# An attention layer fused with a mixture of attention experts: the start and the planner's rules reworked

## The chip, the cores and the metric

The kernel runs on one core of one Trainium2 chip. The metric is the device time of one execution in microseconds (us): 501.53 us before the change, the median of 3 runs (500.11 to 502.16). Five engines work side by side: TensorE (PE in the profile, with PEld for its weight loads), VectorE (DVE), ScalarE (ACT), GpSimd (POOL) and SyncE (SP), which only issues DMAs. ACT issues DMAs too.

## What is computed

Two layers follow each other for each of 8 batches: an attention with 8 heads, 512 local positions and 32 global ones, and a mixture of 4 experts, each of which is a causal attention over the 544 positions.

```python
# 1: attention; local queries see a band of 32 positions on each side, and the 32 global keys
s_g = scale * q_g @ concat(k_g, k_l).T;  out_g = softmax(s_g) @ concat(v_g, v_l)
s_ll = where(|i - j| <= 32, scale * q_l @ k_l.T, -1e9)
out_l = softmax(concat(scale * q_l @ k_g.T, s_ll)) @ concat(v_g, v_l)
x = concat(out_g, out_l), heads side by side        # 8 x 544 x 512

# 2: experts; two of the four are used at each position, by the gate's logits
logits = x @ w_gate;  w = softmax over the two largest
for e in range(4):
    q, k, v = x @ wq[e], x @ wk[e], x @ wv[e]
    out += w[e] * softmax(causal(scale * q @ k.T)) @ v @ wo[e]
```

All is fp32; the experts' products are taken in fp32r with operands split in a high and a low part.

## The kernel before

**Its units.** The attention goes by pairs of heads, four pairs to a batch, 32 pairs in all. A pair k passes through `p1_load` and `p1_load_values` (its keys, queries and values, `kn`, `qn`, `v`), `p1_trans` (keys and queries turned, on TensorE for the first 6 pairs, on DVE afterwards, into `kd` and `qp`), `p1_scores` (L536), `p1_softmax` (L548 on DVE, L551 on ACT), `p1_ptrans` (the weights turned by TensorE, L569), `p1_av` (the value product, L599) and `p1_turn` (L569 again, then `xh` and `xl`, the high and low part of x). Two pairs share the products of the global queries: `p1_global_scores` (L663) and `p1_global_av` (L703). The values need copies of their 32-row blocks to other partitions, `move` and the copies of `vg` in `p1_load_values`; all of them ran on POOL (L279 there).

When the four pairs of a batch are done, the experts follow: `m_v` (L762), `m_qk` (L733), the scores (L854), their turn (L569), the value product `m_av` (L921) and `out_tile` (L1003). `project` puts `m_v` of batch 0 into step 5 and the products of its queries and keys into steps 6 and 7, while the attention of batch 1 goes on.

**What sets the order.** No engine chooses at run time. Each function records operations in a `Plan` with a time that the author wrote down, and `Plan.place` then lays them out, always the one that can start first by its own account; on PE it weighs a penalty for a changed shape of the tile on the array (`CHANGE`) and one for late priority (`PULL`), over all operations within `REACH` of the first one. The priorities are 100 per step s. The order is then fixed, engine by engine, and an engine waits where the order's next operation is not ready.

**What can hold a queue.** A DMA that fills a buffer waits on its issuing engine until the buffer is free, and what is queued behind it waits too. `kn` and `qn` have three buffers each, `v` three, `vg` one; the expert weights come in through the buffers `mptw`, three of them. `setup` loads a weight and splits it in a high and a low part (one copy on ACT or DVE, one subtraction on DVE at L394). `setup_bands` and `setup_masks` build the constants; `load` issues on SP or ACT for the first step and on SP afterwards.

```python
for name, when in (("masks", 3), ("v", 2), ("k", 2), ("q", 3), ("o", 6)):
    if s == when:
        setup(name)
```

## Time and profile before

| | |
|---|---|
| median of 3 runs | 501.53 us (500.11 to 502.16) |
| the profiled execution, its own time | 505.81 us |
| its span, first to last instruction | 504.0 us |
| mean granted TensorE clock | 0.99 |
| chain that ended last | PE 76%, DVE 9%, DMA 4%, "issue" 4%, SP's queue 4%, ACT 3% |
| read from HBM, written to it | 30.42 MB, 8.91 MB |

The profile is of one execution. Its rows give a start or a busy time in us; "x64" is a count of instructions, and the brackets behind a row tell how long the engine had been idle and what ended that, "issue" where no semaphore did. A fp32 product is two matmul records, so that `p1_scores` with 32 matmuls in the program is 64 in the trace. Matmul and weight load are two instructions of one stream.

### The profile page before, as it was taken

To read this page: it belongs to the slowest core of one execution; us is meant where nothing else is said; L and a number is where in the kernel's file an instruction comes from. 1 tells how busy PE (TensorE), PEld (TensorE's weight loads), DVE (VectorE), ACT (ScalarE), POOL (GpSimd) and SP (SyncE) were. 2 spreads that over 40 slices of the span, in tenths; PEclk is the share of its full clock that TensorE was granted. 3 is DMA by queue.
4 is the path that set the end of the run, shared out by engine and by line. 5 is a ranking of instruction groups with operands and counts; after the bars stand their busy time and mean duration, and the time that the engine had idled before them with its cause. 6 is when DMAs were issued, how large, how long until landed. Compare 5 with 4: busy or idle time off the path is not lost.

```text
span 504.0 us, 25622 instructions
## 1 busy us (share of the span) xinstructions
PE 469.3 (93%) x10532; PEld 410.7 (81%) x10532; DVE 385.7 (77%) x1708; ACT 324.4 (64%) x1171; POOL 281.0 (56%) x520
## 2 busy tenths in 40 slices
PE   5787979799999999999989999999999999999985
PEld 3676968589889889889878889898988889888774
DVE  5889768989876997779956998769966976475570
ACT  1668636976756866768746867669757764563662
POOL 5879817869456492928656392837649261331220
PEclk9989989999999999999999999999999999999989
DMA  9955666654246324445146234453022100200203
GB/s 191 220 117 97 140 113 122 115 81 85 35 86 158 68 40 76 106 93 100 32 88 149 49 64 66 108 115 79 4 53 86 28 4 3 85 3 1 86 3 104
DMA packets 181620, 40.98 MB, mean 81 GB/s; under 512 B 176896, under 2 KB 176896, under 8 KB 181504
## 3 DMA queue, kind: packets, MB, share of 16 engines
q1 hardware_dynamic: 169488, 28.70, 31.0%
q10 hardware_dynamic: 12016, 10.65, 6.9%
q8 instruction: 82, 1.34, 1.1%
q14 instruction: 34, 0.28, 0.2%
HBM read 30.42 MB, written 8.91 MB: 78 GB/s over the span
## 4 chain that ended last, share of the span: by engine, by line
PE 76%; DVE 9%; DMA 4%; issue 4%; SPq 4%; ACT 3%; ACTq 1%; POOLq 0%; POOL 0%; DVEq 0%
PE bank L733 18%; PE bank L569 10%; PE bank L1003 9%; PE bank L762 8%; PE bank L921 7%; PE bank L599 6%; PE bank L854 5%; PE bank L536 4%; SPq L295 4%; DVE pm L868 3%; PE bank L703 2%; PE bank L663 2%; DMA qn<-in_q_l_dram 2%; DVE st L548 2%; PE bank L773 1%
## 5 line engine op out<-in xcount | busy, mean ns | idle before, releaser
L886 POOL TENSOR_SCALAR pm<-pm,msm,gate 128x512 f32<-128x512 f32 (+3 forms) x124 | 74.3, 612 | 101.1 <-DVE msm L877 56.1
L279 POOL COPY v<-v 32x512 f32<-32x512 f32 (+1 forms) x192 | 114.5, 596 | 19.8 <-DMA v<-in_v_l_dram 10.0
L551 ACT ACTIVATE st<-st,sm 128x128 f32<-128x128 f32 x256 | 99.7, 392 | 12.3 <-DVE sm L548 12.0
L279 POOL COPY v<-vg 32x640 f32<-32x640 f32 (+1 forms) x96 | 65.3, 680 | 37.6 <-PE bank L703 32.8
L872 ACT ACTIVATE pm<-pm,msm 128x512 f32<-128x512 f32 (+3 forms) x128 | 70.8, 554 | 18.9 <-DVE msm L868 17.8
L548 DVE CUSTOM_DVE_ANT_0 st<-bank,band 128x128 f32<-128x128 f32 x256 | 58.0, 284 | 3.2 <-PE bank L536 3.0
L868 DVE CUSTOM_DVE_ANT_0 pm<-bank,cmask 128x512 f32<-128x512 f32 (+3 forms) x128 | 55.2, 480 | 2.4 <-PE bank L854 2.1
L551 ACT ACTIVATION_READ_ACCUMULATOR st<-st,sm 128x1 f32 x256 | 48.6, 190 | 0.0
L854 PE MATMUL bank<-kt,qt 64*32 64x384 f32 (+3 forms) x1024 | 43.7, 433 | 1.0 <-issue 1.0
L921 PE MATMUL bank<-mptw,vt 128*64 128x128 f32 x640 | 41.0, 281 | 1.7 <-DVE xn L603 0.9
L599 PEld LDWEIGHTS bank<-v,ptw 128*32 128x32 f32 x2048 | 31.3, 112 | 12.8 <-issue 7.7
L536 PE MATMUL bank<-kd,qp 64*32 64x128 f32 x2048 | 39.4, 280 | 2.1 <-issue 2.1
L599 PE MATMUL bank<-v,ptw 128*32 128x64 f32 x2048 | 36.8, 223 | 4.4 <-DVE msm L868 2.5
L277 ACT COPY mptw<-bank 128x384 f32<-128x384 f32 (+1 forms) x50 | 24.2, 520 | 25.6 <-PE bank L921 18.4
L921 PEld LDWEIGHTS bank<-mptw,vt 128*64 128x64 f32 x640 | 36.6, 140 | 3.7 <-issue 2.3
L536 PEld LDWEIGHTS bank<-kd,qp 64*32 64x32 f32 x2048 | 32.1, 108 | 8.6 <-issue 5.0
L733 PE MATMUL bank<-xh,wk_hi 128*128 128x272 f32 x128 | 37.7, 294 | 0.0
L277 ACT COPY ptw<-bank 128x512 f32<-128x512 f32 x34 | 20.0, 594 | 27.1 <-PE bank L569 26.6
L733 PE MATMUL bank<-xl,wk_hi 128*128 128x272 f32 x128 | 37.0, 289 | 0.0
L733 PE MATMUL bank<-xl,wq_hi 128*128 128x272 f32 x128 | 36.9, 288 | 0.0
L733 PE MATMUL bank<-xh,wk_lo 128*128 128x272 f32 x128 | 36.9, 288 | 0.0
L733 PE MATMUL bank<-xh,wq_hi 128*128 128x272 f32 x128 | 36.8, 288 | 0.0
(159 smaller groups left out, 1321.1 us busy)
## 6 DMA issues: line engine op xcount, KB each, us to landing
out_dram<-ot ACTq DMA_DIRECT2D x32, 256.0 KB, 2.1
v<-in_v_l_dram SPq DMA_DIRECT2D x60, 120.0 KB, 2.9
kn<-in_k_l_dram SPq DMA_DIRECT2D x104, 64.0 KB, 2.8
qn<-in_q_l_dram SPq DMA_DIRECT2D x104, 64.0 KB, 2.8
v<-in_v_l_dram SPq DMA_DIRECT2D x31, 64.0 KB, 3.2
kn<-in_k_l_dram SPq DMA_DIRECT2D x8, 128.0 KB, 4.1
qn<-in_q_l_dram SPq DMA_DIRECT2D x8, 128.0 KB, 3.8
ot<-in_q_g_dram SPq DMA_DIRECT2D x8, 64.0 KB, 2.2
```

The source lines that it names most:

```text
L279: ENG[e].tensor_copy(out, in_)
L536: nc.tensor.matmul(sp[h].t[32 * g:32 * g + 32, 128 * t:128 * t + 128], qp.t[rows, 32 * u:32 * u + 32], kd.t[rows, c:c + 128], start=True, ...
L548: op("DVE", 211, lambda e, h=h, t=t, i=i: nc.vector.tensor_tensor_reduce(out=st.t[:, h, t], in0=sp[h].t[:, 128 * t:128 * t + 128], in1=ban ...
L551: op("ACT", 385, lambda e, h=h, t=t, i=i: nc.scalar.activation(st.t[:, h, t], st.t[:, h, t], AF.Exp, bias=sm.t[:, 0, i:i + 1], scale=-1.0, ...
L569: nc.tensor.transpose(two[y].t[:, k, :], block()[rows], ident[rows, rows])
L599: nc.tensor.matmul(xq.t[32 * g:32 * g + 32, t, h, :], pt.t[:, h, 32 * u:32 * u + 32], v.t[:, h, window(u), :], start=True, stop=True)
L733: nc.tensor.matmul(pp.t, w[:, ch, cols], x(part, ch)[:, n], start=(ch == 0 and w is hi and part == 0), stop=(ch == NCH - 1 and part == 1))
L854: nc.tensor.matmul(sp[x].t[32 * u:32 * u + 32, at:at + n], qt.t[rows, q0:q0 + 32], kt.t[rows, :n], start=True, stop=True)
L868: op("DVE", 78 + 1.04 * n, lambda e, x=x, at=at, n=n, i=i, s=s: nc.vector.tensor_tensor_reduce(out=pm.t[:, x, at:at + n], in0=sp[x].t[:, a ...
L872: op("ACT", 280 + 0.83 * n, lambda e, x=x, at=at, n=n, s=s: nc.scalar.activation(pm.t[:, x, at:at + n], pm.t[:, x, at:at + n], AF.Exp, bia ...
L886: lambda e, x=x, at=at, n=n, i=i, s=s: ENG[e].tensor_scalar(pm.t[:, x, at:at + n], pm.t[:, x, at:at + n], sm.t[:, 3, s:s + 1], gate.t[:, i ...
L921: nc.tensor.matmul(yp.t[64 * x:64 * x + 64, 128 * i - n0:128 * i - n0 + 128], vt.t[:, j, 64 * (2 * c + x):64 * (2 * c + x) + 64], flat[:, ...
```

## The change

The planner is changed in four ways. On PE it no longer takes the candidate with the least start time plus penalties, but the one that leaves least time unused, looking one operation further (`waste`, `DEPTH` 1). The penalty for a changed shape falls from 300 to 50 and the reach rises from 130 to 250. `run` keeps account of the instruction stream in blocks of 256, each of which comes a given time after a place in the block before the last. And between 14 and 45 us by its own clock, loads are ordered with less in flight (`FEW`).

```diff
+    def run(self, t, o, state):
+        shape, at, came, then = state
+        ns = o.ns["PE"] * (FILLX if t < SLOW else 1.0)
+        if o.shape != shape:
+            ns += SWITCH.get(shape, 95.0)
+        end, left = t, o.size
+        while left:
+            part = min(left, (LEAD if at < LEAD else BLOCK) - at)
+            end += ns * part / o.size
+            at, left = at + part, left - part
+            if at == LEAD:
+                then = max(end, came) + (FETCH if end > SLOW else FIRST_FETCH)
+            elif at == BLOCK:
+                end, came, at = max(end, came), then, 0
...
+    def waste(self, found, first, now, state, depth):
+        def cost(f):
+            t, o = max(f[0], now), f[1]
+            end, after = self.run(t, o, state)
+            c = end - now - o.ns["PE"] + CHANGE * (o.shape != state[0]) + PULL * (o.prio - first)
...
-                        t = max(t, lanes[0], dma - AHEAD)
+                        t = max(t, lanes[0], dma - (AHEAD if dma < FULL or dma > SLOW else FEW))
```

In the kernel itself six things change.

```diff
-            op("DVE", 1450, f, r=[tri], w=[("band", t)])
+            op("DVE" if t < 2 else "POOL", 1450 if t < 2 else 2200, f, r=[tri], w=[("band", t)])
...
-        op("POOL", 3750, f, w=["masks"])
+        op("POOL", 3750, f, r=[("w", "v")], w=["masks"])
...
+    def warm(after, n, ns):
+        def f(e):
+            nc.tensor.matmul(warm_to.t[:, :128 * n], ident, ident.unsqueeze(1).to_broadcast([128, n, 128]),
+                             start=True, stop=True)
+        op("PE", ns, f, r=after, w=[(warm_to, plan.prio)], size=4)
+    def start_tables():
+        first = buf("sgm", [128, 8], 3)
+        op("ACT", 1300, lambda e: nc.scalar.copy(first.t, ident[:, :8]), w=[first], late=40)
...
-        evac(lambda: kq.t, lambda: pg.t, 256, [pg], [kq])
+        evac(lambda: kq.t, lambda: pg.t, 256, [pg], [kq], "ACT|DVE" if b else "DVE")
...
-            return "POOL", ns
+            return ("POOL|ACT", (ns, 60 + 0.83 * n)) if k < SHARED else ("POOL", ns)
...
+    warm([], 4, 1700)
     p1_batch(0)
...
+    start_tables()
     p1_batch_turn(0)
+    warm([G[0]["pg"]], 1, 430)
     p1_trans(0)
+    warm([PR[0]["px"]], 1, 300)
     setup_bands()
...
-        for name, when in (("masks", 3), ("v", 2), ("k", 2), ("q", 3), ("o", 6)):
+        for name, when in (("masks", 3), ("v", 2), ("k", 2), ("q", 3), ("o", 8)):
```

`warm` multiplies the identity with itself on TensorE, to no use of the result. `start_tables` makes ACT load its function table before its first real work. The first copies out of the banks of pair 0 go to DVE alone, two of the four bands to POOL, and the copies of the values of the first 4 pairs (`SHARED`) may go to ACT. The masks wait for the value weights, so that they are built later. The output weights are loaded in step 8 and not in step 6. The scores, softmax and turning of the first four pairs get the priority of their own pair (`first`).

The planner lays out all 500 us anew. Three places show what the prediction speaks of. The first is TensorE's queue from its start; `ot` holds the global keys and queries, `kd` and `qp` the turned keys and queries. Before:

```order
L420 MATMUL bank_64<-ident,ot 128x64 x4
L506 MATMUL bank_65<-ident,kn 128x128 x4
L506 MATMUL bank_66<-ident,qn 128x128 x4
L506 MATMUL bank_67<-ident,kn 128x128 x4
L506 MATMUL bank_68<-ident,qn 128x128 x4
L536 MATMUL bank_69<-kd_77,qp 32x128
```

and with the change:

```order
L447 MATMUL bank_64<-ident 128x512
L477 MATMUL bank_65<-ident,ot 128x64 x4
L447 MATMUL bank_64<-ident 128x128
L565 MATMUL bank_66<-ident,kn 128x128 x4
L565 MATMUL bank_67<-ident,qn 128x128 x4
L447 MATMUL bank_64<-ident 128x128
L565 MATMUL bank_68<-ident,kn 128x128 x4
L565 MATMUL bank_69<-ident,qn 128x128 x4
L595 MATMUL bank_70<-kd_77,qp 32x128
```

Three products of the identity stand ahead of and between the turns; the first score product still stands behind the turned keys and queries of pair 1.

The second place is SP's queue from the expert weights on (`mptw` is the buffer that they come in through; the first `v` in each piece is that of pair 3, the first `vg` that of batch 1). Before:

```order
L295 DMA mptw<-in_moe_wk_dram 128x8x64 x2
L295 DMA kn<-in_k_l_dram 128x4x64 x2
L295 DMA qn<-in_q_l_dram 128x4x64 x2
L295 DMA mptw<-in_moe_wq_dram 128x8x64 x2
L295 DMA v<-in_v_l_dram 96x5x64 x2
L295 DMA v<-in_v_l_dram 128x2x64
```

and with the change:

```order
L339 DMA mptw<-in_moe_wk_dram 128x8x64 x2
L339 DMA kn<-in_k_l_dram 128x4x64 x2
L339 DMA v<-in_v_l_dram 96x5x64
L339 DMA vg<-in_v_g_dram 32x8x64
L339 DMA v<-in_v_l_dram 96x5x64
L339 DMA v<-in_v_l_dram 128x2x64
L339 DMA qn<-in_q_l_dram 128x4x64 x2
L339 DMA mptw<-in_moe_wq_dram 128x8x64 x2
```

The queries of pair 5 and the query weights have moved behind the values of pair 3 and the global values of batch 1. The first of these waits for a buffer of `v`, which is free when the first global value product (L703) has read the values of pair 0.

The third place is the high part of the output weights, `wo_hi`. Before it was copied on ACT, ahead of the gate's exponential (L830), the copies of projected keys and queries and of turned weights:

```order
L776 COPY vt<-bank_71 32x260
L277 COPY kt<-bank_66 128x272
L277 CAST wo_hi<-mptw 128x1024
L830 ACTIVATE xt<-xt 128x20
L277 COPY kt<-bank_70 128x272
L277 COPY qt<-bank_68 128x272
L277 COPY ptw<-bank_69 128x8x64
```

Now it is copied on DVE, in step 9, behind the turned queries (L578) of pair 9 and between small steps of the experts' softmax:

```order
L935 TENSOR_SCALAR msm<-msm 128x2
L578 STREAM_TRANSPOSE qp<-qn 128x512
L937 RECIPROCAL msm<-msm 128x2
L323 CAST wo_hi<-mptw 128x1024
L928 ISA pm,msm<-bank_71,cmask 128x128
L928 ISA msm 128x1
L438 TENSOR_TENSOR wo_lo<-mptw,wo_hi 128x1024
```

Its DMA now stands on SP behind 95 loads where it stood behind 69. On TensorE the whole order changes too: the expert products of a batch, which stood in runs of four, now stand in ones and twos between the products and turns of the pairs. Counted over the program, the shape of the tile on the array changes 233 times where it changed 178 times, and before the first `m_v` the instruction stream is 2076 instructions long (matmuls, weight loads and semaphore waits) where it was 2169: the score product of pair 6 has moved behind it.

More of the change, by code (lines that the diff above doesn't have):

```diff
@@ L68 @@
 MARGIN = 400.0
-REACH = 130
+REACH = 250
 PULL = 4.0
-CHANGE = 300.0
+CHANGE = 50.0
+THEN = 1.0
+DEPTH = 1
 SOON = 100
+SHARED = 4
+APART = 100
+EARLY = 0
+FILLX = 1.05
+BLOCK = 256
+FETCH = 3650.0
+FIRST_FETCH = 5000.0
+LEAD = 208
 class Plan:
@@ L124, in slot_time @@
         return t
+    def run(self, t, o, state):
[12 more added lines that the diff above has]
+                end, came, at = max(end, came), then, 0
+        if not o.size:
+            end = t + ns
+        return end, (o.shape, at, came, then)
+    def waste(self, found, first, now, state, depth):
[3 more added lines that the diff above has]
+            c = end - now - o.ns["PE"] + CHANGE * (o.shape != state[0]) + PULL * (o.prio - first)
+            if depth:
+                rest = [g for g in found if g is not f]
+                if rest:
+                    c += THEN * self.waste(rest, first, end, after, depth - 1)[0]
+            return c
+        return min(((cost(f), f[1].k, f) for f in found), key=lambda x: x[:2])
     def place(self, log=None):
+        state = (None, BLOCK - 193, 0.0, 0.0)
         free = dict.fromkeys(self.ENGINES, 0.0)
@@ L131, in place @@
         lanes = [0.0] * LANES
-        shape = None
         def enter(o):
@@ L142, in place @@
         left = len(self.ops)
+        last = (None, None)
         while left:
@@ L166, in place @@
                 if e == "PE":
-                    t, o = min(found, key=lambda f: (
-                        f[0] + CHANGE * (f[1].shape != shape) + PULL * (f[1].prio - pe[0].prio), f[1].k))
+                    key = (free[e], tuple((f[0], f[1].k) for f in found))
+                    if key != last[0]:
+                        last = key, self.waste(found, pe[0].prio, free[e], state, DEPTH)[2]
+                    t, o = last[1]
                 else:
@@ L181, in place @@
                     queue[x].remove(o)
-            ns = o.ns[e]
-            if e == "PE" and t < SLOW:
-                ns *= 1.3
-            if e == "PE" and o.shape != shape:
-                ns += SWITCH.get(shape, 95.0)
-                shape = o.shape
-            end = t + ns
+            if e == "PE":
+                end, state = self.run(t, o, state)
+            else:
+                end = t + o.ns[e]
             free[e] = end
@@ L500, in p1_trans @@
         if k < FIRST:
+            engs = "ACT|DVE" if k else "DVE"
             for src in (kn, qn):
-                px = ps([128, SL], "px")
+                px = pr["px"] = ps([128, SL], "px")
                 def f(e, src=src, px=px):
@@ L538, in f @@
                                          start=True, stop=True)
-        op("PE", 885, f, r=[qp, kd], w=sp, shape="scores")
+        op("PE", 885, f, r=[qp, kd], w=sp, shape="scores", size=128)
     def p1_softmax(k):
@@ L569, in f @@
                     nc.tensor.transpose(two[y].t[:, k, :], block()[rows], ident[rows, rows])
-        op("PE", 50 + 62 * n, f, r=r, w=two, shape="turn")
+        op("PE", 50 + 62 * n, f, r=r, w=two, shape="turn", size=4 * n)
         for y in range(2):
@@ L663, in f @@
                             nc.tensor.matmul(to, kq.t[rows, 2 * g + j, SG:], k_, start=True, stop=True)
-            op("PE", 704 - 480 * half, f, r=[kq, *kdl], w=[sp], shape="scores")
+            op("PE", 704 - 480 * half, f, r=[kq, *kdl], w=[sp], shape="scores", size=32)
             op("DVE", 78 + 1.04 * n, lambda e, sp=sp, half=half, n=n: nc.vector.tensor_scalar(
@@ L749, in clear @@
                 nc.gpsimd.memset(vt.t[64:128, 4, :], 0.0)
-            op("POOL", 720, clear, w=[(vt, "clear")])
+            op("POOL", 720, clear, r=[("w", "v")], w=[(vt, "clear")])
             for g in range(NCH // 2):
@@ L855, in f @@
                                          kt.t[rows, :n], start=True, stop=True)
-        op("PE", 20 + 1.68 * sum(128 * (i + 1) for i, _ in TILES[t]), f, r=[kt, qt], w=sp, shape="scores")
+        op("PE", 20 + 1.68 * sum(128 * (i + 1) for i, _ in TILES[t]), f, r=[kt, qt], w=sp, shape="scores",
+           size=32 * len(TILES[t]))
     def m_softmax(b, c, t):
@@ L924, in m_av @@
             op("PE", 214 * sum(i + 1 for i in some), f, r=[vt, *{id(pts[i][0]): pts[i][0] for i in some}.values()], w=[yp],
-               shape="half")
+               shape="half", size=8 * sum(i + 1 for i in some))
             high_low(lambda part, n0=n0, n=n: y[part].t[:, c, n0:n0 + n], lambda yp=yp: yp.t, n, [yp],
@@ L945, in f @@
                                      start=True, stop=True)
-            op("PE", 30 + 1.67 * n, f, r=[*qts, *kts], w=[sp], shape="scores")
+            op("PE", 30 + 1.67 * n, f, r=[*qts, *kts], w=[sp], shape="scores", size=16)
             if half == 0:
@@ L1060, in sooner, with first @@
         if k < NP:
-            plan.prio, then = 100 * k + SOON, plan.prio
+            plan.prio, then = APART * k + SOON, plan.prio
+            f(k)
+            plan.prio = then
+        else:
+            f(k)
+    def first(k, f):
+        if k < NP:
+            plan.prio, then = APART * k, plan.prio
             f(k)
@@ L1083, in local @@
             if at(s):
-                p1_scores(s)
-                p1_softmax(s)
+                first(s, p1_scores)
+                first(s, p1_softmax)
         def experts():
@@ L1119, in step @@
         if at(s + 1):
-            p1_trans(s + 1)
+            first(s + 1, p1_trans)
         if s < LAG:
```

45 lines of the change are left out of this document (26 added, 19 removed).

## The prediction

> **What bounds the kernel now.** First the share of busy time and the stages (each row: the stretch in us, its length, then busy time and count of PE, PEld, DVE, ACT and POOL, the granted clock, the DMA share and GB/s).
>
> ```profile
> PE 469.3 (93%) x10532; PEld 410.7 (81%) x10532; DVE 385.7 (77%) x1708; ACT 324.4 (64%) x1171; POOL 281.0 (56%) x520
> ...
> 0.00:11.00 11.00, 4.82 (x20) 3.36 (x20) 6.77 (x39) 2.12 (x3) 5.53 (x27) 1.00 1.09 187
> 11.00:23.00 12.00, 10.88 (x322) 8.79 (x320) 9.34 (x48) 7.75 (x37) 10.37 (x17) 1.00 1.17 218
> 23.00:32.00 9.00, 5.80 (x142) 5.01 (x142) 6.90 (x31) 5.99 (x23) 7.48 (x13) 0.81 0.77 155
> 32.00:51.00 19.00, 15.87 (x600) 12.65 (x597) 18.23 (x73) 12.86 (x51) 16.26 (x26) 1.00 0.53 96
> ...
> 66.00:75.00 9.00, 5.80 (x194) 5.08 (x196) 6.42 (x19) 3.10 (x9) 1.42 (x3) 0.81 0.61 99
> ...
> 105.00:480.00 375.00, 367.51 (x8132) 324.49 (x8134) 291.64 (x1275) 251.72 (x894) 202.99 (x371) 1.00 0.31 68
> ```
>
> From 105 to 480 us PE stands idle for only 7.5 of 375 us: there only PE's own work counts. What a better start can give lies ahead of that: up to 51 us, where the experts begin, and around 66 to 75, where PE is busy for 5.80 of 9 us. From 32 to 51 VectorE is the full engine, 18.23 of 19.
>
> Next PE's waits (sum in us, times, longest).
>
> ```profile
> PE bank L569 <- DVE xn L603: 3.6, 2, 3.2
> ...
> PE bank L569 <- issue: 2.6, 2, 2.2
> ...
> PE bank L536 <- issue: 2.1, 4, 1.1
> PE bank L599 <- issue: 1.8, 3, 0.8
> ...
> PE bank L984 <- issue: 1.4, 1, 1.4
> ...
> PE bank L854 <- issue: 1.0, 1, 1.0
> ...
> PE bank L703 <- issue: 0.9, 1, 0.9
> ...
> PE bank L921 <- issue: 0.7, 2, 0.5
> ```
>
> The seven rows with "issue" add up to 10.5 us: PE waited for no semaphore. The timeline says where (start, busy time, then the idle time before it).
>
> ```profile
> 11.19 1.96 PE L536 MATMUL bank<-kd,qp 64*32 64x128 f32 x64
> ...
> 25.71 0.34 PE L569 MATMUL bank<-ident,xn 64*128 64x64 f32 x4 [2.19 <-issue]
> ...
> 31.88 0.53 PE L703 MATMUL bank<-v,longt 96*32 96x64 f32 x20 [0.88 <-issue]
> ...
> 35.61 0.44 PE L536 MATMUL bank<-kd,qp 64*32 64x128 f32 x12 [0.26 <-issue]
> ...
> 38.30 0.87 PE L536 MATMUL bank<-kd,qp 64*32 64x128 f32 x41
> 39.78 0.64 PE L536 MATMUL bank<-kd,qp 64*32 64x128 f32 x23 [0.61 <-issue]
> ...
> 51.11 0.39 PE L762 MATMUL bank<-wv_hi,xh 128*128 128x260 f32 x1
> ...
> 69.72 0.46 PE L569 MATMUL bank<-ident,xn 64*128 64x64 f32 x8 [3.20 <-DVE xn L603]
> ```
>
> These waits cut through the middle of an operation: the product that goes on at 31.88 had stopped after 20 of its 40 matmuls, that of 38.30 after 41 of 64. Counted in matmuls and weight loads, they lie 256 instructions apart or a multiple of that. So I read them as PE waiting for its own program, which comes by DMA, to share the rings with the data. The DMA rows of 15 to 30 us and of 30 to 50 us (packets, MB, share) show its pace.
>
> ```profile
> q8 instruction: 3, 0.05, 1.4%
> ...
> q8 instruction: 5, 0.08, 1.8%
> ```
>
> A block of 256 every 5 us in the first, in which the data queue is full, and every 4 us in the second. Without waits, 600 matmuls and their 597 loads ran in 19 us, 4.06 us per 256: PE eats its program about as fast as it comes. The 82 blocks of the whole program (two instructions to each of 10532 matmuls, by 256) are not to be made fewer by this change.
>
> In the Trainium skill, "Runtime: NRT & Kernel Launch", section "Instruction fetch mechanics", the sequencer refills in blocks of 256 instructions by its own DMA queue, and the fetch is hidden, as it issues more slowly than it fills. The spacing agrees; that it is hidden does not, with 2.19 us at 25.71. By that rule the planner's account of blocks would win nothing.
>
> **The change, part by part.**
>
> *Fill: the first expert product (L762, 51.11).* The first scores stand at 11.19, behind the queries of pair 1. These are now issued earlier, behind ACT's table load, so I take the scores 1.5 us earlier. The identity, the first copies on VectorE and the two bands on POOL lie in PE's, VectorE's and POOL's waits for the first data, and I put them at nothing by themselves: PE and VectorE waited for DMAs there. The warm products may raise the clock sooner. The same four turns before and after the clock rose:
>
> ```profile
> 4.55 1.12 PE L506 MATMUL bank<-ident,kn 128*128 128x128 f32 x4 [0.45 <-DMA kn<-in_k_l_dram]
> ...
> 16.26 0.66 PE L506 MATMUL bank<-ident,kn 128*128 128x128 f32 x4
> ```
>
> At 1.12/0.66 for all PE work of 4.5 to 11 us (4.82 us busy at most by the first stage's length) and part of the first scores (1.96 against 1.12 in the row at 222.84 below), at most 2.5 us go; none if the block that comes next sets the pace, as at 25.71. I take 0, the nearest row being that wait. The first copies of pair 0 on VectorE cost at most one 0.6 us copy in a row.
>
> In the Trainium skill, "TensorE: Matmul & The Clock Gate", Part 1 wants about 3.4 us of sustained work for the full clock, while Part 4 has it that transposes don't count as busy as other products do. By Part 4 the warm products would bring up the clock where the turns can't: up to those 2.5 us; by the row at 25.71, nothing. The granted clock of 0.81 in 23 to 32 us, after 3.2 us of PE idle in all, agrees with Part 1; which of the two holds for turns no row tells.
>
> From then on VectorE sets the earliest end: 9.34 + 6.90 + 18.23 = 34.5 us of work from 11 to 51, and by the order its work before the first expert product stays within 1 us of that. From 11 us (scores 1.5 us earlier and their 1.3 us) with 1 us of gaps this gives 46.5. ACT has 7.75 + 5.99 + 12.86 = 26.6 us and gets 16 copies of values from POOL, less the cast of `wk_hi`:
>
> ```profile
> L277 ACT COPY ptw<-bank 128x512 f32<-128x512 f32 x34 | 20.0, 594 | 27.1 <-PE bank L569 26.6
> ...
> L279 POOL COPY v<-v 32x512 f32<-32x512 f32 (+1 forms) x192 | 114.5, 596 | 19.8 <-DMA v<-in_v_l_dram 10.0
> ```
>
> By 594 ns of the nearest ACT copy the 16 are at most 9.5 us, some smaller, less 1.1: 8, so 34.6 from 9.7, or 44.3. POOL falls from 34.1 us by as much and takes the bands early, so it is not last. PE's blocks: 2076 instructions instead of 2169, 93 fewer or 1.5 us at 4.06 us per 256, so 51.11 becomes 49.6 if no wait for a block goes, and earlier with lighter DMA in 14 to 45. From both sides: 51.1 (nothing) and 44.3 (ACT alone). I take 46.5 by VectorE's row, **−4.6**.
>
> What the moved loads add is a wait: SP's loads of pair 3's values stand behind the first global value product, with `vg` of batch 1, the queries of pair 5 and `wq` behind them. Before:
>
> ```profile
> 32.41 4.42 SPq L295 DMA_DIRECT2D v<-in_v_l_dram  x6
> ```
>
> That wait ended at 32.41, when the product at 31.88 was through. The product has moved in PE's stream from instruction 1002 to 1385, and stands before the products of pair 3; before, number 1385 ran at 38.3. If it runs at 33, as the 46.5 implies, nothing is late; if at 38.3, `v`, the queries of pair 5 and `wq` are 6 us late, and the gain is gone (rival 2).
>
> *Output weights two steps later.*
>
> ```profile
> 64.57 1.05 ACT L277 CAST wo_hi<-mptw 128x1024 fp32r<-128x1024 f32 x1 [4.53 <-DMA mptw<-in_moe_wo_dram]
> ```
>
> ACT stood 4.53 us for a load that was still under way, the gate's exponential behind it; VectorE's gates and `xn` followed, and PE stood 3.20 us at 69.72. Then the clock: 0.81 over the 9 us from 66, a loss of 0.19 x 9 = 1.7. Now VectorE casts in step 9, with more steps between its load and its use than before. Both go: **−4.9**. If the cast again waits for its load, VectorE stands in ACT's place, at most 3 us of it back; the other end is −4.9 in full, since the work of the cast is the same.
>
> *Steady state.* One score product moved behind the first expert product: +1.1 by its row (222.84). Then 55 more changes of shape (178 to 233). Pairs of rows:
>
> ```profile
> 185.36 1.13 PE L854 MATMUL bank<-kt,qt 64*32 64x512 f32 x14
> 186.42 1.10 PE L599 MATMUL bank<-v,ptw 128*32 128x64 f32 x64
> 187.45 0.65 PE L569 MATMUL bank<-ident,pm 64*128 64x64 f32 x13
> ...
> 221.96 1.09 PE L854 MATMUL bank<-kt,qt 64*32 64x512 f32 x16
> 222.84 1.12 PE L536 MATMUL bank<-kd,qp 64*32 64x128 f32 x63
> ...
> 227.80 1.10 PE L599 MATMUL bank<-v,ptw 128*32 128x64 f32 x64 [0.50 <-DVE msm L868]
> 228.72 0.75 PE L703 MATMUL bank<-v,longt 128*32 128x64 f32 x40
> ```
>
> A score product to the next operation of another shape: 186.42 − 185.36 = 1.06; to one of the same: 0.88. A value product to another shape: 1.03, to the same: 0.92. So 0.11 to 0.18, about 0.15 each, 8.3 us for 55 if all is exposed, 0 if every one lies in a stretch that waits for the next block anyway. PE's share of 98% speaks for the first, the pace of 4.06 us per block for the second; I take half, +4. The waits for blocks: 10.5 us less the 3.9 of the four before 51 leave 6.6; an order that alternates short and long operations may spare up to all of them, or none; 2 by choice, −2. Together **+3.1**.
>
> Sum: −4.6 − 4.9 + 3.1 = −6.4, or 499.4 in the profiled execution's 505.8. That one stands 4.3 above the median of 501.5, so the median forecast is **495.1**, given as 495.0. The tail keeps its order: nothing.
>
> **The rivals.**
>
> 1. *Slower: the shape changes in full.* The looser order spends 0.15 on each of 55 changes (+8.3), no wait for a block is spared, and a product comes behind (+1.1). The fill gives only the earlier queries (−1.5), the output weights −4.9. Sum +3.0: 504.5 in the median. For it speaks that PE is 98% busy, so there is little to hide under; against it that half of its blocks come no faster than it eats. It decides from about 0.10 us a change (even) and 0.14 (slower by 0.5%). Chance 0.13.
>
> 2. *The fill does nothing.* The first global value product comes at 38.3, its place in the stream, and the values of pair 3 behind it; the first expert product stays at 51. Output weights −4.9, steady state +3.1: 499.7. For it speaks 38.30 as the row of that place and VectorE's 18.23 of 19; against it that SP's wait then hits pair 3 only after its scores. Chance 0.14.
>
> 3. *Better.* Blocks come every 4 us from 15 us on, since the loads are spaced, PE meets none of its waits, and the fill ends by ACT's bound plus a little, −6.5; the changes are half hidden (+4), the 6.6 are all spared, the score product +1.1; output weights −4.9. Sum −12.9, or 488.6; with the changes all hidden 484.6. For it speak 4.06 us per block in 32 to 51; against it VectorE's 34.5 us, which leave no room for it. Chance 0.15.
>
> Forecast as summed: 0.58. That the loads in 14 to 45 us are paced too far, so that keys come late, would show as PE waiting for `kn` and belongs to rival 2.
>
> **How the numbers follow.** Half a per cent, 2.5 us, is about what a measurement of this kernel can tell from no change. Faster: the forecast and rival 3, 0.73; same: rival 2, 0.14; slower: rival 1, 0.13. The range, 486 to 504, takes in rival 2 and rival 3 as summed, and leaves out rival 1 and what lies below 486.
>
> **What would show it.** The first row of L762: 46.5, or 51. PE's "issue" waits: fewer than 3.9 us before it, and instruction packets of 15 to 30 us: 4 instead of 3. PE's idle time at 66 to 75 us and the clock there: both gone, unless the `wo_hi` cast on VectorE shows idle time ended by its load. SP's row of `v` at 33 or at 38. For rival 1: from 105 to 480 the same work in more time with PE as busy as ever, and starts after a change of shape 0.15 later. The prediction is wrong if the first 51 us are as long as before while the output weights still wait, or if the steady state costs more than the start gains.

## The result, and the profile after

| | before | after |
|---|---|---|
| median, first measurement | 501.64 us (500.11 to 502.16, 4 runs) | 507.57 us (505.49 to 508.24, 4 runs) |
| ratio, 95% interval | | 1.0116 [1.008, 1.0153] |
| median, measured again later | 501.95 us (22 runs) | 505.52 us (8 runs) |
| ratio, 95% interval | | 1.0068 [1.0041, 1.0095] |
| profiled execution, own time | 505.81 us | 508.24 us |

The change makes the kernel slower, by 0.7 to 1.2%. The forecast was 495, with 486 to 504 as its range.

From the page of the kernel after, the busy times and the program's own DMA queue:

```profile
PE 479.4 (95%) x10538; PEld 414.2 (82%) x10538; DVE 387.5 (77%) x1714; ACT 325.2 (64%) x1163; POOL 276.6 (55%) x523
...
q8 instruction: 83, 1.36, 1.2%
```

PE is busy for 10.1 us more than before (469.3). The three products of the identity are 3.5 us of this (2.08, 0.79 and 0.64), and a part is the lower clock of this execution (0.975 in the mean, before 0.990); the rest is the same work that takes longer. In a second profile of each kernel (a_again and b_again below) PE is busy for 474.8 and 471.6 us. The stages of the first one (columns as in the prediction):

```profile
11.00:23.00 12.00, 9.43 (x281) 7.41 (x274) 9.90 (x64) 11.83 (x39) 10.02 (x18) 0.86 1.02 194
23.00:32.00 9.00, 6.27 (x224) 5.08 (x202) 6.53 (x35) 8.36 (x36) 0.32 (x1) 1.00 0.54 108
32.00:51.00 19.00, 14.53 (x392) 12.55 (x395) 14.86 (x51) 14.48 (x50) 12.59 (x29) 0.73 0.56 105
...
66.00:75.00 9.00, 7.75 (x256) 6.92 (x255) 6.99 (x42) 5.60 (x27) 1.84 (x5) 1.00 0.63 102
...
105.00:480.00 375.00, 368.87 (x8082) 321.43 (x8079) 292.52 (x1294) 240.26 (x863) 205.47 (x375) 1.00 0.31 66
```

VectorE, which was to set the end of the fill, is no longer full in 32 to 51 us (14.86 of 19), POOL stands in 23 to 32 (0.32 of 9), and the clock is 0.73 where it was 1.00. PE's waits:

```profile
PE bank L565 <- DMA kn<-in_k_l_dram: 2.8, 2, 2.5
PE bank L658 <- POOL v L323: 2.6, 2, 2.4
PE bank L628 <- issue: 2.3, 2, 2.1
PE bank L658 <- issue: 1.8, 1, 1.8
PE bank L762 <- issue: 1.6, 2, 1.4
...
PE bank L595 <- issue: 1.3, 1, 1.3
PE bank L1044 <- issue: 1.2, 1, 1.2
```

The wait for `xn` is 0.6 us instead of 3.6 and "issue" is 8.2 us instead of 10.5 (in the second profiles 9.9 and 9.8), but POOL's copies of values are a new wait, and keys a larger one. Where, in PE's timeline:

```profile
9.76 1.16 PE L595 MATMUL bank<-kd,qp 64*32 64x128 f32 x64
...
16.26 0.97 PE L565 MATMUL bank<-ident,kn 128*128 128x128 f32 x4 [2.52 <-DMA kn<-in_k_l_dram]
...
27.59 0.27 PE L628 MATMUL bank<-ident,long 64*128 64x64 f32 x1 [2.15 <-issue]
...
35.17 0.32 PE L762 MATMUL bank<-v,longt 128*32 128x64 f32 x2
...
44.14 0.42 PE L658 MATMUL bank<-v,ptw 128*32 128x64 f32 x2 [2.36 <-POOL v L323]
...
52.03 0.39 PE L821 MATMUL bank<-wv_hi,xh 128*128 128x260 f32 x1
```

The first scores came at 9.76, as forecast (9.7). The first global value product came at 35.17, not at 33 (before, its first half ran at 30.49), and the first expert product at 52.03, not at 46.5. What stood behind that product is seen on POOL:

```profile
36.63 1.38 POOL L323 COPY v<-vg 32x640 f32<-32x640 f32 x2 [12.77 <-PE bank L762]
38.07 0.53 POOL L392 MEMSET cmask<- 128x512 f32 x1
...
41.83 1.48 POOL L323 COPY v<-vg 32x640 f32<-32x640 f32 x2
43.37 1.38 POOL L323 COPY v<-v 32x640 f32<-32x640 f32 x2
```

and on SP:

```profile
23.83 3.19 SPq L339 DMA_DIRECT2D kn<-in_k_l_dram  x2
36.63 0.33 SPq L339 DMA_DIRECT2D v<-in_v_l_dram  x1
```

SP issues nothing from 27.0 to 36.6, POOL stands for 12.8 us, then builds the masks (38.07 to 41.83) ahead of the next copies of values, and PE waits for these at 44.14.

### The profile page after: what moved, and what is told of

The parts are those of the page before. It is cut to its first block, busy times and chain, and to the rows that moved or that the text cites. A ratio compares the mean times of both kernels' runs of the same rounds, so it can differ in the third digit from the quotient of the medians.

```text
span 506.4 us, 25650 instructions
## 1 busy us (share of the span) xinstructions
PE 479.4 (95%) x10538; PEld 414.2 (82%) x10538; DVE 387.5 (77%) x1714; ACT 325.2 (64%) x1163; POOL 276.6 (55%) x523
## 4 chain that ended last, share of the span: by engine, by line
PE 86%; DVE 5%; DMA 3%; issue 3%; ACT 1%; POOL 1%; ACTq 1%; SPq 0%; POOLq 0%; DVEq 0%
PE bank L792 20%; PE bank L628 11%; PE bank L821 10%; PE bank L1063 9%; PE bank L913 7%; PE bank L658 6%; PE bank L981 6%; PE bank L595 6%; PE bank L722 3%; DMA qn<-in_q_l_dram 2%; PE bank L762 2%; PE bank L832 2%; PE bank L1004 1%; DVE st L607 1%; PE bank L1044 1%
## 5 line engine op out<-in xcount | busy, mean ns | idle before, releaser
L323 POOL COPY v<-v 32x512 f32<-32x512 f32 (+3 forms) x181 | 108.4, 599 | 28.2 <-DMA v<-in_v_l_dram 19.2
L946 POOL TENSOR_SCALAR pm<-pm,msm,gate 128x512 f32<-128x512 f32 (+3 forms) x125 | 76.7, 630 | 81.5 <-DVE msm L937 41.2
L323 POOL COPY v<-vg 32x640 f32<-32x640 f32 (+1 forms) x91 | 61.7, 678 | 54.9 <-PE bank L762 47.9
L913 PE MATMUL bank<-kt,qt 64*32 64x384 f32 (+3 forms) x1024 | 45.7, 445 | 0.0
L658 PE MATMUL bank<-v,ptw 128*32 128x64 f32 x2048 | 38.0, 226 | 5.8 <-POOL v L323 2.6
L658 PEld LDWEIGHTS bank<-v,ptw 128*32 128x32 f32 x2048 | 32.1, 113 | 10.1 <-issue 3.8
L595 PE MATMUL bank<-kd,qp 64*32 64x128 f32 x2048 | 38.3, 279 | 1.3 <-issue 1.3
L792 PE MATMUL bank<-xh,wq_hi 128*128 128x272 f32 x128 | 38.6, 302 | 0.2 <-ACT kt L321 0.2
L981 PE MATMUL bank<-mptw,vt 128*64 128x128 f32 x640 | 38.5, 275 | 0.0
L821 PE MATMUL bank<-wv_hi,xh 128*128 128x260 f32 x128 | 37.3, 291 | 0.0
L792 PE MATMUL bank<-xh,wq_lo 128*128 128x272 f32 x128 | 37.0, 289 | 0.0
L595 PEld LDWEIGHTS bank<-kd,qp 64*32 64x32 f32 x2048 | 30.3, 108 | 7.7 <-issue 4.4
```

The source lines that it names most:

```text
L323: ENG[e].tensor_copy(out, in_)
L595: nc.tensor.matmul(sp[h].t[32 * g:32 * g + 32, 128 * t:128 * t + 128], qp.t[rows, 32 * u:32 * u + 32], kd.t[rows, c:c + 128], start=True, ...
L658: nc.tensor.matmul(xq.t[32 * g:32 * g + 32, t, h, :], pt.t[:, h, 32 * u:32 * u + 32], v.t[:, h, window(u), :], start=True, stop=True)
L792: nc.tensor.matmul(pp.t, w[:, ch, cols], x(part, ch)[:, n], start=(ch == 0 and w is hi and part == 0), stop=(ch == NCH - 1 and part == 1))
L821: nc.tensor.matmul(pv.t, x(part, ch)[:, 128 * i:128 * i + 128], w[:, ch, :], start=(ch == 0 and part == 0 and w is hi), stop=(ch == NCH - ...
L913: nc.tensor.matmul(sp[x].t[32 * u:32 * u + 32, at:at + n], qt.t[rows, q0:q0 + 32], kt.t[rows, :n], start=True, stop=True)
```

## The experiments

Ratios are to runs of the kernel before on the same chip (22 to 31 runs each time, medians 501.95 to 502.4). The chip differs from run to run, so ratios are to be compared, not medians. One kernel's runs lie 2 to 4 us to either side of its median, and a profile is of one of them. The last two columns are the start, in us, of the first global value product (L703 before, L762 after) and of the first expert product (L762 before, L821 after) in the run's own profile. An edit to the program makes the planner lay out the whole order anew, except in a_busy, a_mute and a_nfl_mute, which keep the order of the run that they change.

| run | median us | ratio, 95% interval | first global value product | first expert product |
|---|---|---|---|---|
| b_again: before, unchanged | 502.82 | 1.0008 [0.9979, 1.0037] | 28.65 | 54.05 |
| b_wo8: before, output weights in step 8 | 502.62 | 1.0004 [0.9973, 1.0035] | 30.48 | 51.2 |
| b_c0: before, penalty 0 | 504.99 | 1.0056 [1.0029, 1.0082] | 25.88 | 49.0 |
| b_newrules: before, new rules | 504.63 | 1.0042 [1.0013, 1.0071] | 27.89 | 47.2 |
| b_newfill: the same, old rules from 45 us on | 502.58 | 1.0024 [0.9996, 1.0053] | 27.84 | 46.5 |
| a_again: after, unchanged | 505.52 | 1.0068 [1.0041, 1.0095] | 34.35 | 51.1 |
| a_oldlater: after, old rules from 45 us on | 506.14 | 1.0082 [1.0051, 1.0113] | 34.31 | 50.3 |
| a_oldrules: after, old rules throughout | 503.62 | 1.003 [1.0002, 1.0059] | 28.43 | 53.9 |
| a_busy: after, PE kept busy in three waits | 507.57 | 1.0089 [1.0055, 1.0124] | 34.83 | 50.2 |
| a_v4: after, four buffers of values | 509.76 | 1.0141 [1.0096, 1.0186] | 35.00 | 49.1 |
| a_masks: after, masks early | 505.89 | 1.0082 [1.0054, 1.011] | 28.61 | 49.7 |
| a_nofirst: after without `first` | 502.95 | 1.0029 [1.0, 1.0058] | 33.10 | 49.8 |
| a_nowarm: after without `warm` | 503.96 | 1.0035 [1.0009, 1.0061] | 28.97 | 51.2 |
| a_nf_later: without `first`, old rules later | 504.63 | 1.0072 [1.0041, 1.0102] | 33.45 | 47.8 |
| a_nfnw_later: the same without `warm` | 501.78 | 0.999 [0.9962, 1.0019] | 28.95 | 50.2 |
| a_nfnw: without `first` and `warm`, new rules | 506.29 | 1.0091 [1.0056, 1.0126] | 28.79 | 49.6 |
| a_mute: after, `warm` planned but not issued | 504.79 | 1.0062 [1.0037, 1.0087] | 34.48 | 50.4 |
| a_nfl_mute: a_nf_later, the same | 505.24 | 1.0045 [1.0021, 1.007] | 33.19 | 48.9 |

**Is it the clock?** The profile after has four stretches at half clock in its first 100 us, before had two. Two runs.

b_again is before without an edit.

> The kernel before, unchanged, for a second profile. Its first profile (505.81 us by itself) lay 4.2 us above the median of its runs (501.6), with three stretches of 3.4 us at half clock. Clock theory (the change is slower because PE spends 23.9 us at half clock in the profile after, where it was 10.2 us): a run of 501.6 shows one or two such stretches less, at 1.7 us each. Shape theory (57 more changes of shape cost 0.15 us each): the clock says nothing here, and a run of 501.6 has the same stretches at half clock and less idle time.

Its profiled execution took 503.81 us, 2.0 less than the first, with a lower clock in its fill. One row of its stages:

```profile
32.00:51.00 19.00, 16.11 (x506) 13.06 (x504) 16.61 (x66) 12.19 (x48) 15.85 (x24) 0.77 0.56 103
```

0.77 here, 0.87 from 51 to 66, and 1.00 in both in the first profile: in this pair, more half clock goes with less time. The pair isn't clean, as the first execution has a wait of 3.20 us at 69.72 besides, and b_again is 2.9 us behind it at the first expert product. a_busy:

```diff
+    def busy(to, n):
+        for _ in range(n):
+            nc.tensor.matmul(to, ident, ident.unsqueeze(1).to_broadcast([128, 4, 128]), start=True, stop=True)
...
+                    if k == 3 and src is kn:
+                        busy(px.t, 2)
...
+            busy(xq.t.rearrange("p t h d -> p (t h d)"), {3: 1, 4: 2}.get(k, 0))
```

> The changed kernel, with products of the identity (128x512) put at the head of three operations whose inputs were late, in the bank that they write anyway: two ahead of the turned keys at 16.26, one ahead of the value product at 32.70, two ahead of that at 44.14 (it goes through the first 2.36 us idle). PE is busy in these waits and nothing else changes. Clock theory: the half-clock stretches from 16.4, 33.5 and 43.7 (13.7 us in all) go, the first expert product comes at 48 to 49.5 and not at 52.0, and the kernel takes 503 to 505. Shape theory or waits alone: 52 and 507.6, within 1 us.

The wait at 44 in its timeline:

```profile
41.02 1.13 PE L453 MATMUL bank<-ident 128*128 128x512 f32 x2
43.95 0.30 PE L664 MATMUL bank<-v,ptw 128*32 128x64 f32 x2 [1.57 <-POOL v L323]
44.62 1.02 PE L664 MATMUL bank<-v,ptw 128*32 128x64 f32 x57 [0.37 <-POOL v L323]
```

The value product then takes 1.02 us, not the 1.81 of the changed kernel: the clock stays up there (0.91 from 32 to 51 us instead of 0.73). The first expert product comes at 50.23, 1.8 us earlier than in the first profile and short of the 48 to 49.5 of the clock theory, and the time is the rival's.

That doesn't clear the clock altogether. The granted clock is known for every execution, and in the 131 executions of before that the ratios rest on, a straight line gives 2.0 us less for each 0.01 more of mean clock (correlation −0.52). These have 0.990 in the mean, the twelve of the changed kernel 0.981; by that line, an estimate, 1.9 of the 3.9 us between their means go with the clock. Against it stands a_busy again: its ten executions have 0.990, as before has, and it is 0.9% slower. So the clock alone isn't the cause; its share stays open, since the waits that come ahead of a lower clock (2.19 us at 25.71, 3.20 at 69.72) cost time themselves.

**Do the output weights wait?** b_wo8 changes `("o", 6)` to `("o", 8)` in before.

> Before, with the output weights loaded in step 8 and nothing else changed. Forecast's step: the 3.20 us idle at 69.7 and the half clock behind it go, -4.9 us, 496.7. Rival (the wait is only replaced, or the planner's other order gives it back): within 1 us of 501.6.

No difference, and the interval leaves no room for 4.9 us: the rival. Two rows say why; first the same cast in b_again, then in b_wo8:

```profile
63.28 1.05 ACT L277 CAST wo_hi<-mptw 128x1024 fp32r<-128x1024 f32 x1
```

```profile
74.65 1.05 ACT L277 CAST wo_hi<-mptw 128x1024 fp32r<-128x1024 f32 x1 [5.94 <-DMA mptw<-in_moe_wo_dram]
```

In a second execution of before ACT does not wait at all, and PE has no idle time at 69.7: the 4.53 us and what hung on them belonged to one of the two profiled executions. And where ACT does wait for 5.94 us, in b_wo8, PE shows no wait behind it.

**What holds the fill?** Seven runs on its parts. a_masks and a_nofirst take back one edit each:

```diff
-        op("POOL", 3750, f, r=[("w", "v")], w=["masks"])
+        op("POOL", 3750, f, w=["masks"])
```

> The changed kernel, in which the masks no longer wait for the value weights: POOL builds them in its idle time of 12.8 us ahead of 36.6, and not from 38.07 to 41.83, between the copies of the values of pairs 3 and 4. Theory (this is what holds the value product at 44.14): its 2.36 us idle go, the first expert product comes at 49 to 50.5 and not at 52.0, and the kernel at 504 to 506. Rival (the loads behind the first global value product hold it): 51.5 to 52.5, 507 to 508.

```diff
-                first(s, p1_scores)
-                first(s, p1_softmax)
+                p1_scores(s)
+                p1_softmax(s)
...
-            first(s + 1, p1_trans)
+            p1_trans(s + 1)
```

> The changed kernel, with the scores, softmax and turns of the first four pairs at the priority of their step again. Theory (taking the scores of pair 3 at 21.9 instead of 34.3 puts them ahead of the value products, so that the first global one, which frees the buffer of values, comes at 35.2): the first global value product at 31 to 33, the first expert product at 48 to 50, 504 to 506. Rival: 51 to 53, 507 to 508.

a_nowarm leaves out the three calls of `warm`.

> The changed kernel without the three products of the identity at its start. If they do as they are meant, the clock rises later and the first expert product comes 1 to 2.5 us later than 52.0; by the forecast (they lie in waits and what they gain is taken by the next block) the time stays within 1 us of 507.6.

a_v4 gives the values a fourth buffer:

```diff
-        gn = buf("ot", [64, H, D], 4)
+        gn = buf("ot", [64, H, D], 2)
...
-        v = buf("v", [128, 2, NW + 1, D], 3)
+        v = buf("v", [128, 2, NW + 1, D], 4)
...
-        both = buf("turned", [128, 2, D], 2)
+        both = buf("turned", [128, 2, D], 1)
...
-        ot = buf("ot", [128, DM], 4)
+        ot = buf("ot", [128, DM], 2)
```

> The changed kernel with four buffers of values instead of three (the room comes from the buffers of the output tiles, two instead of four, and of the turned global rows, one instead of two). Theory of the fill: SP and POOL no longer stand from 24 to 36.6 us for the first global value product, the values of pair 3 are there in time, the 2.36 us idle at 44.14 goes, and the first expert product comes at 47 to 49 and not at 52.0. Rival (VectorE or the blocks hold the fill anyway): 51 to 53. The whole time says less here, since the later order is laid out anew: 502 to 508.

b_newfill goes by the new rules to 45 us (`free[e] < SLOW`) and by the old ones after:

> The kernel before, laid out by the new rules up to 45 us of the planner's time and by the old ones after, none of the kernel's edits. 164 changes of shape, as before. Theory (the new rules help the fill, which the profile of the rules alone showed with the first expert product at 47.2, and cost only afterwards by their changes): first expert product at 47 to 49, steady stage 395 to 398, 497 to 500. Rival (the old rules after a new fill cost too, as with the edits, where it was 506.1): 503 to 506.

The first global value product and the first expert product of a_masks:

```profile
28.61 0.75 PE L762 MATMUL bank<-v,longt 128*32 128x64 f32 x40
...
42.60 0.40 PE L658 MATMUL bank<-v,ptw 128*32 128x64 f32 x2 [2.51 <-POOL v L323]
...
49.72 0.39 PE L821 MATMUL bank<-wv_hi,xh 128*128 128x260 f32 x1
```

and of b_newfill:

```profile
27.84 0.77 PE L767 MATMUL bank<-v,longt 128*32 128x64 f32 x40
...
46.48 0.39 PE L826 MATMUL bank<-wv_hi,xh 128*128 128x260 f32 x1
```

These two go as the forecast thought: the first global value product comes before 30, and the expert products start 2.3 and 5.6 us earlier than at 52.03. Over the table that doesn't hold. b_again, a_oldrules and a_nowarm have the one at 28.4 to 29.0 and the other at 51.2 to 54.05; a_nf_later has 33.45 and 47.8. And executions of one order differ by as much as most of these runs do: 51.11 and 54.05 in the two of before, 52.03, 51.07 and 50.37 in after, a_again and a_mute. So nothing here shows what sets the first expert product.

Nor does that product say when the kernel ends: 46.5 goes with 500.9 in its own execution (the lowest of that run's ten; their median is 502.6), 47.8 with 504.3, 49.1 with 510.6, 53.9 with 501.7.

a_masks has the product and the time of its theory, but not by its way: the wait for POOL's copies of values is still there, 2.51 us at 42.60, and the kernel is no faster than a_again. POOL clears `vt` ahead of these copies, from 38.17 on (L807, L808); the change makes these clears wait for the value weights too, as it does the masks. In a_v4 SP issues the values of pair 3 at 28.41, but POOL still stands 10.7 us for the first global value product, which stays at 35.0. The first expert product comes at 49.15, and the kernel is the slowest of all; its output tiles, with which the global keys and queries share their buffers, have two buffers less, which wasn't tried alone. a_nofirst has the 49.8 that was expected, and at 502.95 less time than the 504 to 506. a_nowarm, expected within 1 us of 507.6, took 504.0: a miss, also against the 505.5 of a_again.

a_mute and a_nfl_mute keep the order and leave the products of the identity out:

```diff
-            nc.tensor.matmul(warm_to.t[:, :128 * n], ident, ident.unsqueeze(1).to_broadcast([128, n, 128]),
-                             start=True, stop=True)
+            pass
```

> The changed kernel in its own order, word for word, only that the three products of the identity are not issued (the planner still counts them). Layout theory (they cost by the order that is laid around them, not by themselves): within 1 us of the changed kernel, 505 to 507, the first global value product at 34.5 to 36.5 again. If the products themselves cost (PE, clock, blocks): 502 to 504.

> The run without the earlier priority and with the old rules later (504.6), in its own order, its three products of the identity not issued. Layout theory: 504 to 506. If the products themselves cost: 501.5 to 502.5, the time of the run that was planned without them (501.8).

Both are as with them (1.0062 and 1.0068; 1.0045 and 1.0072): the products cost nothing that these runs can tell, which is some 2 us. What a_nfnw_later gained (0.999 where a_nf_later has 1.0072) it gained by the other order that the planner laid out without them, and so did a_nowarm, if its 0.3% is a gain.

**What do the changes of shape cost?** b_c0 is before with one number changed, `CHANGE = 300.0` to `CHANGE = 0.0`.

> Before, with the penalty for a changed shape set from 300 to 0 and nothing else: by the planner's own log 252 changes of shape where there were 164, the same products. Shape theory, at 0.11 us a change (what the batches of the changed kernel show: 24 to 28 changes a batch and 3.9 us beyond the sum of the planner's own durations and the idle time, where before has 17 and 2.9): +9.7, less a few us of waits for blocks that fall, 508 to 512. Rival (changes are hidden, or cost only where a block is late): within 2 us of 502.3.

It is slower by 2.8 us: less than the 6 to 10 of the shape theory, more than the 2 of its rival. The stretch from the first expert product of batch 1 to that of batch 7 shows why. In it the same products run, but for what the order moves over its ends. The stretch in before, after and b_c0:

```profile
101.39:436.35 334.96, 327.47 (x7536) 291.49 (x7533) 268.98 (x1194) 230.69 (x834) 194.65 (x358) 1.00 0.34 71
```

```profile
99.78:442.56 342.78, 336.65 (x7617) 294.04 (x7613) 275.26 (x1229) 228.22 (x828) 202.09 (x372) 1.00 0.35 72
```

```profile
90.63:435.54 344.91, 342.45 (x7776) 292.59 (x7773) 274.18 (x1236) 238.30 (x854) 202.13 (x371) 1.00 0.34 73
```

The same for other runs. "Products" is the sum of the durations that the author wrote beside the products of the stretch, which serves to compare its contents; changes are counted in the planner's log, which has 164 and 221 in all.

| run | changes | stretch | PE idle | PE busy | products | busy less products |
|---|---|---|---|---|---|---|
| before | 101 | 335.0 | 7.5 | 327.5 | 310.3 | 17.2 |
| b_again | 101 | 332.8 | 5.7 | 327.2 | 310.3 | 16.9 |
| a_nfnw_later | 101 | 334.2 | 7.0 | 327.3 | 310.3 | 17.0 |
| a_nfnw | 153 | 340.2 | 5.0 | 335.2 | 311.1 | 24.1 |
| after | 157 | 342.8 | 6.1 | 336.7 | 312.0 | 24.7 |
| a_again | 157 | 343.1 | 7.1 | 336.0 | 312.0 | 24.0 |
| b_c0 | 171 | 344.9 | 2.5 | 342.5 | 315.2 | 27.3 |

(24.0 − 17.0)/56 = 0.125 us for a change in a_again, (27.3 − 17.0)/70 = 0.147 in b_c0; a_nfnw has (24.1 − 17.0)/52 = 0.137. (The profile of a_again is taken, since that of after has a stretch at half clock in it, at 197.3 us.) This puts all the added time down to the changes; three different orders give nearly the same price. It is there, and nearly in full. In b_c0 some 4 us of it come back as PE waits less for its program (2.5 us idle); in the changed kernel next to nothing does.

Four pairs have the same fill rules and edits, and other rules from 45 us on: after and a_oldlater, a_nofirst and a_nf_later, b_newrules and b_newfill, a_nfnw and a_nfnw_later. a_oldlater is:

```diff
-                        if o.prio > pe[0].prio + REACH:
+                        if o.prio > pe[0].prio + (REACH if free[e] < SLOW else 130):
...
-                        last = key, self.waste(found, pe[0].prio, free[e], state, DEPTH)[2]
+                        last = key, (self.waste(found, pe[0].prio, free[e], state, DEPTH)[2] if free[e] < SLOW else min(
+                            found, key=lambda f: (f[0] + 300.0 * (f[1].shape != state[0])
+                                                  + PULL * (f[1].prio - pe[0].prio), f[1].k)))
...
```

> The changed kernel, with the old rules of choice on PE (penalty 300, reach 130, no look ahead, no account of blocks) from 45 us of the planner's time on: same fill, some 60 changes of shape less after it. Shape theory: 8 us less than the changed kernel's 507.6, about 500. Clock theory: the fill with its three half-clock stretches stays, first expert product still at 52, and only what those stretches at 91 and 197 us cost can go: 502 to 506, with the time in 300 to 480 us down by no more than 2.

> The changed kernel without the earlier priority of the first pairs' scores, and with the old rules from 45 us on: the fill of the run without that priority (502.95), the 162 changes of shape of the old rules. Layout theory (the fill costs some 3 to 4 us, the changes net 1 to 2): 501 to 503, at least 3 below the same with the priority (506.1). If the 506.1 came from the old rules behind a new fill: 505 to 507.

> The same without the products of the identity as well. Layout theory: the first global value product at 31 to 33, 500.5 to 502.5, the lowest so far and at best 0.3% below before. If the warm products help by themselves: 1 to 2 more than with them.

> The fill of the run of 501.8 (no earlier priority, no products of the identity), with the new rules also after 45 us: 221 changes of shape instead of 162. Three such pairs so far gave 505.5 to 507.6 against 506.1, 503.0 against 504.6, and 504.6 against 502.6. If the changes net nothing (0.1 us each, given back in waits for blocks): within 1.5 us of 501.8. If they cost 2: 503.5 to 504.5.

The ratios of the pairs, new rules less old: −0.1% (+0.3% with the first measurement of after), −0.4%, +0.2% and +1.0%. The last pair is the shape theory's, the second goes against it, and a_oldlater, at 506.1, is just above what either of its theories had. In the profiles from the first product of batch 1 to PE's last row, the new rules took 395.2 to 402.5 us (400.1 in the mean of ten profiles) and the old ones 394.9 to 398.6 (396.6 in nine): 3.5 us, which the ratios show only in part. a_nf_later alone would have given 501 to 503 by the layout theory, and gave 504.6: a miss.

A pattern shows up only when the runs are sorted afterwards, by the first global value product in their profile and by the rules from 45 us on (without b_c0 and a_v4, which change something else). Mean ratios:

| first global value product | old rules later | new rules later |
|---|---|---|
| before 31 us | 1.001 (5 runs) | 1.006 (4 runs) |
| after 33 us | 1.007 (3 runs) | 1.006 (4 runs) |

A late product and the new rules go with some 0.5 to 0.6% each, and with no more together: the new rules lose where the product is early, which is where the pairs have +0.2% and +1.0%. That is a sorting after the fact, of runs that differ in other edits too, and no test; why the two don't add up stays open.

Last, one half of the change each: b_newrules has the rules without the edits, a_oldrules the edits without the rules.

> The kernel before, laid out by the new rules (look ahead, account of blocks, penalty 50, reach 250, spaced loads), without the edits of the kernel (warm products, tables, bands, masks, copies, priorities, output weights). 229 changes of shape where before has 164. Shape theory: 506 to 509, as the steady stage from the first product of batch 1 on takes 400 us or more where before took 395 to 397. Rival (it is the kernel's edits that cost): 500 to 503.

> The edits of the kernel, laid out by the old rules. 163 changes of shape. Shape theory: steady stage as before, 395 to 398 us, and what the fill gains, 0 to 2 us, stays: 500 to 503. Rival (the edits cost, as where only the stage after 45 us went by the old rules, 506.1): 505 to 507.

+0.42% and +0.30%: each half costs a little, less than its theory or its rival would have it, and no half gains. a_again is the whole once more:

> The changed kernel again, for a second profile and more runs. Its time so far, 507.6, is of 4 runs. Layout theory (its own fill, not the clock of one execution, holds it): first global value product at 34.5 to 36.5 again, POOL idle from 24 on again, first expert product at 51 to 53, 506 to 508. If the first profile was an unlucky execution: product at 33, 504 to 505.

Its PE and POOL rows repeat those of the first profile:

```profile
34.35 0.23 PE L762 MATMUL bank<-v,longt 128*32 128x64 f32 x2
...
43.37 0.42 PE L658 MATMUL bank<-v,ptw 128*32 128x64 f32 x2 [2.77 <-POOL v L323]
...
51.07 0.39 PE L821 MATMUL bank<-wv_hi,xh 128*128 128x260 f32 x1
```

```profile
35.27 1.86 POOL L323 COPY v<-vg 32x640 f32<-32x640 f32 x2 [10.76 <-PE bank L762]
```

The late product and the standing POOL are the layout's. The time is 2 us lower than in the first four runs, between the two expectations; 0.7%, of more runs, is the better figure of the two.

No run is faster than before. The best, a_nfnw_later, is level with it.

## Why the prediction was wrong, by its own steps

- **Output weights, −4.9: 0.** This step failed first. The wait was in the trace, and its consequences were read rightly, but a second execution doesn't have it, and moving the load alone changes nothing (1.0004, interval to 0.9973). It may also have been counted twice: the forecast took 4.9 off the profiled 505.8 and then another 4.3, because that execution lay above the median. The wait may well have been part of why it lay there; the execution without it took 503.8.
- **Fill, −4.6: about −1 at the first expert product, and nothing that can be seen at the end.** The sum took VectorE as full from 11 us on, with 1 us of gaps. In the profile after it is busy for 31.3 of the 40 us from 11 to 51 (before 34.5): it waited too. The forecast said that the gain hangs on the first global value product at 33, and is gone at 38.3. It came at 35.17 and 34.35. SP and POOL stood for it, SP issued the values of pair 3 at 36.63 and 35.26 where it had at 32.41, and the first expert product stood at 52.0 and 51.1, against 51.1 and 54.0 in the two profiles of before: rival 2, with half its delay. The masks, moved behind the value weights, were costed at nothing, under POOL's idle time; they came after that time, between its copies of values. That they set PE's wait for these isn't shown: with the masks early it stays. The blocks of the program came no faster either: 3 packets in 15 to 30 us where the forecast looked for 4. The deeper fault is the mark, as the first expert product doesn't tell the end.
- **Steady state, +3.1: +5 in the profiles.** The price of a change, 0.15, was nearly right (0.125 to 0.147), and so was their number (56 in the stretch). That half would be hidden (+4 of 8.3) was the mis-sized term: 7 are in PE's busy time. That waits for blocks would fall by 2 did not come: PE's idle time in the stretch is 6.1 and 7.1, where it was 7.5 and 5.7. The 6.6 us of such waits left behind 51 us were 5.7, since a fifth one lay ahead, 0.84 us at 20.52. From the first product of batch 1 to PE's last row after takes 401.2 and 401.6 us, before 397.3 and 395.1. This part is rival 1's, which decided by exactly this price. Its 504.5 is also the nearest of the summed times, partly by luck: it holds the −4.9 that did not come.
- **Products of the identity, 0: right.** The first scores took 1.16 us in the first profile after, 1.96 in that of a_again, and 1.81 in a_mute without them, so the clock is up in time in one execution of two, for 0.8 us. By the Trainium skill, "TensorE: Matmul & The Clock Gate", Part 4, turns don't count as busy as other products do; whether that is so, these rows don't tell, since with the products the clock was still down at 9.61 in a_again. Nor does the row that the prediction read as agreeing with 3.4 us tell much: the clock of before fell at 26.07, behind 2.19 us of idle time and not 3.2.
- **First scores 1.5 us earlier: right** (9.76 and 9.61, from 11.19). The products of the identity have no part in it: without them a_mute has the scores at 9.83.

In the profiles the account closes, as it must: 3.1 us ahead at the first product of batch 1 (98.4 in the mean, from 101.5), 5.2 lost behind it, 2.2 in all, as the profiled times have it (508.24 and 505.79 against 505.81 and 503.81, means 507.0 and 504.8). Some 0.9 us of both figures is one value product that moved behind this mark, and b_wo8, which gains nothing, is there at 99.2. The medians differ by 3.6 to 5.9, as both profiles of before are above its median. Where its other executions are faster isn't seen in any profile here, and stays open. So the price of the changes is shown, and that the gains did not come; what makes the whole slower by 0.7% is shown in part.

## What to carry to other kernels

A wait that one profile shows is priced only when a second execution has it too, and a step isn't taken off an execution that lay high because of that step. On an engine that is 98% busy, take an added cost per instruction or change of shape in full; what the waits give back is measured, not assumed. An earlier milestone isn't an earlier end: b_newfill's profile is 4.6 us ahead of before at the first expert product, and its median is 0.6 above before's. And where two executions of one order differ by 3 us at a mark, one profile of each kernel can't tell a difference of 2.

## What the hardware showed that was not expected

A lower clock goes with less lost time than PE's work alone would lose. The shortest stretch at half clock in these traces is 3.41 us, in which PE's work loses 1.7. It lowers the mean clock of 502 us by 0.0034, and by the line over 131 executions that goes with some 0.7 us, an estimate. In one pair it even went the other way: b_again ran 32 to 66 us at 0.77 and 0.87 and took 2.0 us less than the execution that ran them at 1.00 and waited later.

And an order laid out anew can move the kernel by some 3 us whatever the edit means: from 0.999 to 1.0045 between two orders that the planner laid out without and with three products, which were issued in neither.
